# Hash attention and a gated feed-forward on one core: a hash ahead of scores, a norm's products on another engine, turns and hashes at other steps

## The chip, the core and the metric

The kernel runs on one core of a Trainium2 chip. The core has a matrix engine (PE; its weight loads are listed apart as PEld), a vector engine (DVE), a scalar engine (ACT), GpSimd (POOL) and a sync engine (SP), which here only issues DMAs. Each works through its own list of instructions in the order of the program; semaphores hold an instruction until what it needs is there. The metric is the device time of one execution in microseconds.

## What is computed

Two parts follow each other. The first is attention with a mask from hashing: each query and each key of 64 numbers is projected on 6 directions, the 6 signs make a bucket, and a query sees only the keys of its own bucket. The second is a feed-forward with a norm ahead of it, a gate and a value.

```python
q_bits = (einsum('bhsd,dk->bhsk', q, proj) > 0)      # q, k, v: 4 x 8 x 768 x 64
k_bits = (einsum('bhsd,dk->bhsk', k, proj) > 0)      # proj: 64 x 6
mask = q_bucket[:, :, :, None] == k_bucket[:, :, None, :]
scores = where(mask, q @ k.T / sqrt(64), -1e9)
x = softmax(scores) @ v                              # to 3072 x 512
xn = x / sqrt(mean(x * x) + 1e-6) * rms_g
out = (silu(xn @ w_gate) * (xn @ w_val)) @ w_out     # 512 -> 1536 -> 512
```

## The kernel before, in words

**Units and steps.** The 3072 tokens are eight units `u` of 384 (`HALF`), two for each batch `b`. A unit has 8 heads, in four pairs `hp`. One step is a third of a head's scores for one unit: two matmuls into a bank pair (`scores`, L321) and one exponential on ACT (`probs`, L333). There are 24 steps to a unit (`NS`), 192 in all. In step `t` the program issues the scores of step `t + 1`, the exponential of step `t`, and then whatever the table `plan[t]` holds, in the order in which it was put there with `at(w, s, f, ...)`. So the order on every engine is written out by hand: `plan` decides, and each engine follows its own share of it. Scores have two buffers, so those of step `t + 1` wait for the exponential of step `t - 1`. The first ten heads in `order` are two of u = 0, two of u = 1, then the other six of u = 0; the rest follow unit by unit.

**Keys and queries.** A pair's q and k come in naturally and are turned, either by PE (`turn_pe`, L150, copied out of its bank by DVE or ACT, L152) for batch 0 and the pairs (1,0) and (1,1), or by DVE block transposes (`turn_dve`, L176 and L183) for the rest. POOL casts them to 16 bits (L166, L196). The hash projects the turned tensors on PE (`d_ps`; L229 in `hash_pairs`, L204 in `hash_half`), DVE takes the signs (`bits`, L212), and they are put below q and k as further rows of the 16-bit operand `QK`, so that one matmul gives score and mask at once. They get there by DVE copies (`move`, L251) or by DMAs from SP (`send`, L258 and L261; `hash_one`, L219 and L280). The dictionary `spots` lists, for each pair that DVE turns, the step of its load, the steps of the turns of k and q (each a part), and the step of its hash.

**Attention and norm.** `av` (L346) multiplies the probabilities with v into `o_ps`, which has one buffer per pair of heads. `attn_out` adds a correction and copies out (DVE, `otmp`, L360), takes the reciprocal (L365), scales (POOL, `x`, L367) and squares (POOL, `sq`, L372). `sumsq` sums the squares (DVE, L376). `norm` adds up the four pairs (`ss`, L386), takes the power -1/2 on POOL (`rstd`, L390) and scales into 16 bits on DVE (`xn`, three instructions, L393). `turn_x` transposes on PE (`x_ps`, L400) and multiplies by the norm's weights on DVE (`xnT`, L406).

**Feed-forward.** `gate` and `value` (`feed`, L417) go through 12 tiles of 128 columns; ACT takes a tanh (L425), DVE two products (`a` and `ht`, L434 and L435). `project` (L446) sums into `y_ps`, `store` copies it out on ACT (L458) and issues the DMA (L459). `spread` distributes these pieces and the hashes that are due over a unit's 24 steps by fixed costs. The banks of `t_ps`, `d_ps`, `x_ps`, `g_ps`, `v_ps` and `y_ps` are three in all, of one tag.

**Zeros.** `idle` (L517) multiplies zeros: matmuls whose result nobody reads. There are eight ahead of the first work, three ahead of the first hash, two ahead of the first scores, two ahead of the second head's hash, and four in steps 37 and 38.

**DMA order.** SP takes its DMAs in the program's order, loads, sends and stores alike. Loaded tiles share a ring of eight buffers, so a load can wait for the last reader of an older tile.

Of the kernel before, what the change touches and what calls it, by code (L numbers as in the profile page):

```python
# [15 lines left out]
H = 8  # L16
# [15 lines left out]
def kernel(  # L32
# [12 lines left out]
    nc = tc.nc  # L45
# [114 lines left out]
    def turned(b, hp, which):  # L160
        return (qT if which == "q" else kT)[b, hp].rearrange("p (h c) -> p h c", h=2)
# [48 lines left out]
    def signs(bt, ps, c0, n):  # L210

        nc.vector.tensor_scalar(  # L212
            out=bt[0:n, 1, c0 : c0 + HALF], in0=ps[0:n], scalar1=0.0, scalar2=0.5,
            op0=ALU.is_gt, op1=ALU.subtract,
        )
# [21 lines left out]
    def hash_direct(b, hp, heads):  # L237


        where = [(which, hh) for which in "kq" for hh in heads]  # L240
        pss = hash_pairs([turned(b, hp, which)[:, hh, :] for which, hh in where])
        bt = spool.tile([128, 2, S], FP16, name="bits")

        def sign(e):
            signs(bt[:, :, e * HALF :], pss[e], 0, 32 * len(where))

        def move(e, kinds="kq", n=1, only=heads):
            for t, (which, hh) in enumerate(where):
                if which in kinds and hh in only:
                    o = (0 if which == "q" else S) + e * HALF  # L250
                    nc.vector.tensor_scalar_mul(  # L251
                        QK[b, 2 * hp + hh, "h"][64:KROWS0, o : o + n * HALF],
                        bt[32 * t : 32 * t + 6, 1, e * HALF : (e + n) * HALF],
                        4.0 * BIT * BIT if which == "k" else 1.0,
                    )

        def send():
            nc.vector.tensor_scalar_mul(bt[:, 0, :], bt[:, 1, :], own)  # L258
            for t, (which, hh) in enumerate(where):
                o = 0 if which == "q" else S  # L260
                nc.sync.dma_start(  # L261
                    out=QK[b, 2 * hp + hh, "h"][64:KROWS0, o : o + S],
                    in_=bt[32 * t : 32 * t + 6, 0, :],
                )

        return sign, move, send
# [47 lines left out]
    def scores(u, i):  # L314
        b, half = divmod(u, 2)
        h, ch = divmod(i, 3)
        rows = KROWS0 if (b, h // 2) in ONPE else KROWS
        ps = scps.tile([128, 2, 512], FP32, name="s_ps")
        for j in range(2):
            jt = 2 * ch + j  # L320
            nc.tensor.matmul(  # L321
                ps[:, j, 0:HALF],
                QK[b, h, "h"][0:rows, S + jt * 128 : S + (jt + 1) * 128],
                QK[b, h, "h"][0:rows, half * HALF : (half + 1) * HALF],
                start=True, stop=True,
            )
        sps[u, i] = ps
# [23 lines left out]
                skip_group_check=True,  # L351
            )

    def attn_out(u, hp):
        b = u // 2
        if hp == 0:
            x[u] = xpool.tile([128, 3, DMODEL], FP32, name="x")
        o = ot.pop((u, hp))
        tmp = spool.tile([128, 3, 2, 66], FP32, name="otmp")
        nc.vector.tensor_add(  # L360
            tmp[:, :, :, 0:65], o[:, :, :, 0:65],
            cvb[b % 2][:, 2 * hp : 2 * hp + 2, 0:65].unsqueeze(1).to_broadcast([128, 3, 2, 65]),
        )
        r = spool.tile([128, 3, 2, 1], FP32, name="rcp")
        nc.vector.reciprocal(r, tmp[:, :, :, 64:65])  # L365
        xd = x[u][:, :, 128 * hp : 128 * hp + 128]
        nc.gpsimd.tensor_mul(  # L367
            xd.rearrange("p c (h d) -> p c h d", h=2), tmp[:, :, :, 0:64],
            r.to_broadcast([128, 3, 2, 64]),
        )  # L370
        sq = spool.tile([128, 3, 128], FP32, name="sq")
        nc.gpsimd.tensor_mul(sq, xd, xd)  # L372
        return sq

    def sumsq(u, hp, sq):
# [4 lines left out]

    ht, gts = {}, {}

    def norm(u):

        ss = spool.tile([128, 3], FP32, name="ss")
        nc.vector.tensor_reduce(  # L386
            out=ss, in_=ssp[u % 2].rearrange("p h c -> p c h"), op=ALU.add, axis=AX.X
        )
        rstd = spool.tile([128, 3], FP32, name="rstd")
        nc.gpsimd.tensor_tensor(out=rstd, in0=ss, in1=mhalf, op=ALU.pow)  # L390
        xn[u] = npool.tile([128, 3, DMODEL], FP16, name="xn")
        for c in range(3):
            nc.vector.tensor_scalar_mul(xn[u][:, c, :], x[u][:, c, :], rstd[:, c : c + 1])  # L393
# [119 lines left out]
    def idle(n, new=None):  # L513

        ps = new("z_ps") if new else wz
        for _ in range(n):
            nc.tensor.matmul(ps, zeros16[:, 0:128], zeros16, start=True, stop=True)  # L517
# [17 lines left out]
    def at(w, s, f, *a):  # L535
        plan[NS * w + s].append(lambda: f(*a))
# [3 lines left out]
    turn_pe(0, 0, 0, "q", act=(0,))  # L540
    cast_part(0, 0, "k", 1, 0, 1)
    turn_pe(0, 0, 1, "k")
    idle(3)
    sign, move, _ = hash_direct(0, 0, (0,))
    turn_pe(0, 0, 1, "q", nc.scalar.copy)
    idle(2)
# [4 lines left out]
    sign(1)  # L551
    move(1, "k")
    scores(0, 0)


    def second_head():
        idle(2)
        sign1, move1, _ = hash_direct(0, 0, (1,))
        sign1(0)
        move1(0)  # L560
        sign1(1)
        move1(1, "k")
        move(1, "q")
        move1(1, "q")

    moves = {}

    def hash_pair(b, hp):
        sign, *moves[b, hp] = hash_direct(b, hp, (0, 1))
        sign(0)  # L570
        sign(1)

    def move_pair(b, hp, hh):
        moves[b, hp][0](0, n=2, only=(hh,))
# [1 line left out]
    def send_pair(b, hp):  # L576
        moves[b, hp][1]()

    at(0, 0, second_head)
    at(0, 1, v_prep, 0, 0)  # L580
    at(0, 1, cast_part, 0, 0, "q", 1)
# [26 lines left out]
    for hp, ts in ((0, (8, 22, 23, 24, 25, 24, 26, 26, 28, 42)), (1, (12, 27, 28, 29, 30, 29, 41, 32, 33, 43))):  # L608
        tl, ts = ts[0], ts[1:]
        for w in "kq":  # L610
            at(0, tl, load_natural, nc.sync, 1, hp, w)
        at(0, tl, load_v, nc.sync, 1, hp)
        at(0, ts[0], new_pair, 1, hp)
        for t, hh, w in zip(ts[0:4], (0, 1, 0, 1), "kkqq"):
            at(0, t, turn_pe, 1, hp, hh, w)
        at(0, ts[4], cast_pool, 1, hp, "k")
        at(0, ts[5], cast_pool, 1, hp, "q")
        at(0, ts[6], hash_pair, 1, hp)
        at(0, ts[7], send_pair, 1, hp)
        at(0, ts[8], v_prep, 1, hp)  # L620
        at(2, 3 + 6 * hp, v_mean, 1, hp, 2, range(6))

    spots = {
# [10 lines left out]
    }  # L634
    sqs = {}

    def o_step(u, hp):
        sqs[u, hp] = attn_out(u, hp)

    def s_step(u, hp):  # L640
        sumsq(u, hp, sqs.pop((u, hp)))

    at(0, 24, nc.gpsimd.tensor_scalar_mul, gcol, gcol, float(DMODEL) ** 0.5)
    at(0, 36, norm, 0)
    at(0, 37, idle, 2, bank)
    at(0, 38, idle, 2, bank)
    for c in range(3):
        at(0, 38, turn_x, 0, c)
    for n, (u, h) in enumerate(order):
        for part in range(2):  # L650
            at(0, 3 * n + 4 + part, av, u, h, part)
        if h % 2:
            at(0, 3 * n + 5, o_step, u, h // 2)
            at(0, 3 * n + (10 if h < 7 else 8 if u == 0 else 7), s_step, u, h // 2)

# [30 lines left out]
    for u in range(7):  # L686
        gates = [
            (FEED, f is gate and part == 0, [(0, f, u, ft, part)])
            for ft in range(NF) for f in (gate, value) for part in range(2)
        ]  # L690
        if u == 0:
            t0 = 40
            spread(t0, 2 * NS - t0, gates)
            continue
        t0 = NS * (u + 1)
        at(0, t0 + 4, norm, u)
        pieces = []
        for i in range(9):
            c, n = divmod(i, 3)
            steps = [(0, project, u - 1, c, 4 * n, 4 * n + 4)]  # L700
            if n == 2:
                steps.append((1, store, u - 1, c))
            pieces.append((4 * PROJ, True, steps))
            if i in (6, 7):
                pieces += [
                    (TURN, False, [(0, turn_x, u, c)]) for c in ((0,), (1, 2))[i - 6]
                ]
        spread(t0, NS, pieces + gates)
# [86 lines left out]
```

## Time and profile before

| What | Value |
|---|---|
| Time, median of 3 runs | 346.39 us (346.1 to 346.78) |
| The profiled execution | 346.98 us, span of its instructions 345.2 us |
| PE busy | 331.2 us, 96% of the span |
| DVE, ACT, POOL busy | 249.8, 225.7, 147.8 us |
| Chain that ended last | PE 80%, DVE 9%, POOL 4%, issue 4%, ACT 2% |
| Exponential, 128x768 (L333) | 192 times, 899 ns each |
| Scores matmul (L321) | 384 times, 326 ns each |
| Scale on POOL (L367) / square on POOL (L372) | 32 times each, 829 / 826 ns |
| Sum of squares on DVE (L376) | 32 times, 528 ns |

A row of the timeline has the start in the span, the length, the engine, the line, the operation, the tiles written and read, and how many alike follow each other; in square brackets stands how long the engine was idle before it and who ended that. The lengths of matmuls overlap, since they are pipelined: what one costs is the distance between starts. A row of the waits has the total, the number and the longest. "Issue" is time for which the profile shows no wait.

### The profile page before, as it was taken

Reading aid. Unit: us, or ns where it says so; the run is one execution under the profiler, and the core shown is the slowest. Engines: PE = TensorE matmul, PEld = TensorE weight load, DVE = VectorE, ACT = ScalarE, POOL = GpSimd, SP = SyncE. Lnnn points to the kernel's source line nnn. Section 1 sums busy time; section 2 is a strip of 40 time slices with the busy share of each in tenths; the row PEclk is TensorE's granted clock in tenths of the full one; section 3 lists DMA queues with packets and bytes.
Section 4 is the critical chain, followed back from the end, with each engine's and each line's share of the span. In section 5 each row is a group of like instructions: output and inputs, shape, how many; then the busy total and the mean of one; then the engine's idle time right before and its main releaser. Section 6 shows DMA issues by size and latency. Waiting matters only on the chain.

```text
span 345.2 us, 7819 instructions
## 1 busy us (share of the span) xinstructions
PE 331.2 (96%) x3035; PEld 198.6 (58%) x3035; DVE 249.8 (72%) x521; ACT 225.7 (65%) x327; POOL 147.8 (43%) x210
## 2 busy tenths in 40 slices
PE   8798978998999999999899999999999999999996
PEld 4455745654656556565556556565556656664554
DVE  2669967777798857987798757988796546674870
ACT  2689984666566667776577767776667767863322
POOL 4389966306354443637453623646460121112000
PEclk9999999999999999999999999999999999999999
DMA  7899955910276925270827016200200010001002
GB/s 248 279 201 293 202 113 75 211 41 30 34 179 98 186 69 104 73 140 10 162 82 133 9 65 116 59 7 9 93 6 4 3 61 32 2 0 63 31 0 93
DMA packets 79029, 31.21 MB, mean 90 GB/s; under 512 B 64928, under 2 KB 75024, under 8 KB 78992
## 3 DMA queue, kind: packets, MB, share of 16 engines
q1 hardware_dynamic: 75888, 25.73, 30.9%
q0 software_dynamic: 2656, 4.72, 7.8%
q8 instruction: 24, 0.39, 0.5%
q10 hardware_dynamic: 448, 0.27, 0.2%
q14 instruction: 13, 0.11, 0.1%
HBM read 28.32 MB, written 6.29 MB: 100 GB/s over the span
## 4 chain that ended last, share of the span: by engine, by line
PE 80%; DVE 9%; POOL 4%; issue 4%; ACT 2%; DVEq 0%; POOLq 0%
PE v_ps L417 17%; PE g_ps L417 17%; PE s_ps L321 15%; PE y_ps L446 13%; PE o_ps L346 9%; PE t_ps L150 2%; PE d_ps L204 2%; PE d_ps L229 2%; PE x_ps L400 2%; DVE xn L393 2%; PE z_ps L517 1%; ACT psb L333 1%; DVE bits L212 1%; POOL rstd L390 1%; POOL x L367 1%
## 5 line engine op out<-in xcount | busy, mean ns | idle before, releaser
L333 ACT ACTIVATE psb<-s_ps,ebias 128x768 f16<-128x768 f32 x192 | 168.1, 899 | 29.8 <-PE s_ps L321 28.5
L321 PE MATMUL s_ps<-QK 76*128 76x384 f16 (+1 forms) x384 | 93.6, 326 | 3.6 <-ACT psb L333 1.2
L425 ACT ACTIVATE t<-g_ps 128x384 f32<-128x384 f32 x96 | 47.1, 490 | 57.7 <-PE g_ps L417 56.9
L417 PE MATMUL g_ps<-xnT,wg 128*128 128x384 f16 x384 | 82.1, 325 | 0.1
L417 PE MATMUL v_ps<-xnT,wv 128*128 128x384 f16 x384 | 80.9, 325 | 0.2 <-DVE a L434 0.2
L367 POOL TENSOR_TENSOR x<-otmp,rcp 128x384 f32<-128x384 f32 x32 | 26.5, 829 | 113.1 <-DVE rcp L365 112.6
L434 DVE SCALAR_TENSOR_TENSOR a<-t,g_ps 128x384 f32<-128x384 f32 x96 | 52.6, 548 | 25.3 <-ACT t L425 23.4
L446 PE MATMUL y_ps<-wo,ht 128*128 128x512 f16 x276 | 68.0, 378 | 0.0
L346 PEld LDWEIGHTS <-psb 128*128 128x128 f16 x1152 | 51.8, 97 | 20.8 <-issue 5.0
L435 DVE SCALAR_TENSOR_TENSOR ht<-a,v_ps 128x384 f16<-128x384 f32 x96 | 53.2, 554 | 11.0 <-PE v_ps L417 1.9
L346 PE MATMUL o_ps<-vl,psb 128*128 128x65 f16 x1152 | 56.3, 193 | 2.6 <-DVE otmp L360 2.5
L321 PEld LDWEIGHTS <-QK 76*128 76x128 f16 (+1 forms) x384 | 34.3, 98 | 34.9 <-issue 9.3
L417 PEld LDWEIGHTS <-wv 128*128 128x128 f16 x384 | 35.2, 97 | 22.4 <-issue 1.6
L417 PEld LDWEIGHTS <-wg 128*128 128x128 f16 x384 | 34.7, 97 | 21.1 <-DVE xnT L406 0.6
L446 PEld LDWEIGHTS <-ht 128*128 128x128 f16 x276 | 24.7, 97 | 22.5
L372 POOL TENSOR_TENSOR sq<-x 128x384 f32<-128x384 f32 x32 | 26.4, 826 | 2.5
L458 ACT COPY ysb<-y_ps 128x512 f32<-128x512 f32 x23 | 13.5, 585 | 18.5 <-PE y_ps L446 18.4
L376 DVE TENSOR_REDUCE ssp<-sq 128x3 f32<-128x384 f32 x32 | 16.9, 528 | 10.6 <-POOL sq L372 10.4
L360 DVE TENSOR_TENSOR otmp<-o_ps,cvb 128x390 f32<-128x390 f32 x32 | 17.9, 558 | 8.3 <-PE o_ps L346 8.1
L196 POOL CAST QK<-qT 64x768 f16<-64x768 f32 x20 | 16.6, 832 | 16.7 <-DVE qT L183 15.3
L196 POOL CAST QK<-kT 64x768 f16<-64x768 f32 x20 | 16.7, 833 | 13.9 <-DVE kT L183 9.2
L393 DVE TENSOR_SCALAR xn<-x,rstd 128x512 f16<-128x512 f32 x24 | 14.1, 643 | 7.8 <-POOL rstd L390 7.8
(74 smaller groups left out, 279.5 us busy)
## 6 DMA issues: line engine op xcount, KB each, us to landing
vn<-in_v_dram SPq DMA_DIRECT2D x16, 384.0 KB
out_dram<-ysb SPq DMA_DIRECT2D x23, 256.0 KB
qL<-in_q_dram SPq DMA_DIRECT2D x40, 96.0 KB
kL<-in_k_dram SPq DMA_DIRECT2D x40, 96.0 KB
kn<-in_k_dram SPq DMA_DIRECT2D x5, 384.0 KB
qn<-in_q_dram SPq DMA_DIRECT2D x5, 384.0 KB
wg<-in_moe_w_gate_dram POOLq DMA_DIRECT2D x2, 768.0 KB, 9.7
wv<-in_moe_w_val_dram POOLq DMA_DIRECT2D x2, 768.0 KB, 9.6
```

Source lines behind the costliest of these rows:

```text
L196: nc.gpsimd.tensor_copy(QK[b, 2 * hp + hh, "h"][0:64, o : o + S], src[64 * hh : 64 * hh + 64, :])
L321: nc.tensor.matmul(ps[:, j, 0:HALF], QK[b, h, "h"][0:rows, S + jt * 128 : S + (jt + 1) * 128], QK[b, h, "h"][0:rows, half * HALF : (half + ...
L333: nc.scalar.activation(psb[u, h][:, 2 * ch : 2 * ch + 2, :], sps.pop((u, i))[:, :, 0:HALF], AF.Exp, bias=ebias, scale=ESCALE,)
L346: nc.tensor.matmul(o[:, c, hh, 0:65], psb[u, h][:, jt, c * 128 : (c + 1) * 128], vls[b % 2][:, h, 2 * (jt % 3) + jt // 3 if b in PARITY el ...
L367: nc.gpsimd.tensor_mul(xd.rearrange("p c (h d) -> p c h d", h=2), tmp[:, :, :, 0:64], r.to_broadcast([128, 3, 2, 64]),)
L372: nc.gpsimd.tensor_mul(sq, xd, xd)
L393: nc.vector.tensor_scalar_mul(xn[u][:, c, :], x[u][:, c, :], rstd[:, c : c + 1])
L417: nc.tensor.matmul(ps, w[:, kt, fs], xnT[u][:, kt, :], start=(kt == 0), stop=(kt == 3))
L425: nc.scalar.activation(t, fbank[u, ft, "g_ps"], AF.Tanh, scale=0.5)
L434: nc.vector.scalar_tensor_tensor(out=a, in0=t, scalar=1.0, in1=g, op0=ALU.add, op1=ALU.mult)
L435: nc.vector.scalar_tensor_tensor(out=ht[u][:, ft, :], in0=a, scalar=0.5, in1=vv, op0=ALU.mult, op1=ALU.mult)
L446: nc.tensor.matmul(y, ht[u][:, ft, c * 128 : (c + 1) * 128], wo[:, ft, :], start=(ft == 0), stop=(ft == NF - 1),)
```

## The change

1. *The start.* One zero instead of three ahead of the first hash. The second head's hash matmuls are issued straight behind the first scores; the two zeros ahead of it are gone.
2. *The first norm.* For the last pair of u = 0, `attn_out` scales and squares on DVE; the sum of squares, the total and the power follow at once, in step 32, behind the attention matmuls. The hash of pair (1,1) moves behind them, from step 32 to 33, its signs after the total, its send from 33 to 34. `xn` is formed in step 33's list, the transposes stand in step 37 instead of 38, with three zeros instead of four, and the gates of u = 0 begin in step 38 instead of 40.
3. *Turns and hashes.* (1,2): turns in steps 48 and 49 instead of 48 to 51, hash at 50 instead of 52. (2,0) and (2,1) are loaded two steps earlier. (2,3): turns from 96, 96, 97, 97, 99, 99, 105, 105 to 96, 97, 99, 105, 105, 106, 106, 107, hash from 106 to 108. (3,3) likewise 48 steps later. (3,0): turns up to two steps later, hash at 118 instead of 117.

```diff
-    def attn_out(u, hp):
+    def attn_out(u, hp, eng=nc.gpsimd):
...
-        nc.gpsimd.tensor_mul(
+        eng.tensor_mul(
             xd.rearrange("p c (h d) -> p c h d", h=2), tmp[:, :, :, 0:64],
             r.to_broadcast([128, 3, 2, 64]),
         )
         sq = spool.tile([128, 3, 128], FP32, name="sq")
-        nc.gpsimd.tensor_mul(sq, xd, xd)
+        eng.tensor_mul(sq, xd, xd)
...
-    def norm(u):
+    rstds = {}
+
+    def norm_scale(u):
...
         nc.gpsimd.tensor_tensor(out=rstd, in0=ss, in1=mhalf, op=ALU.pow)
+        rstds[u] = rstd
+
+    def norm(u):
+        if u not in rstds:
+            norm_scale(u)
+        rstd = rstds.pop(u)
...
-    idle(3)
+    idle(1)
     sign, move, _ = hash_direct(0, 0, (0,))
...
     scores(0, 0)
+    sign1, move1, _ = hash_direct(0, 0, (1,))
     def second_head():
-        idle(2)
-        sign1, move1, _ = hash_direct(0, 0, (1,))
         sign1(0)
...
-        at(0, ts[6], hash_pair, 1, hp)
-        at(0, ts[7], send_pair, 1, hp)
+        if hp == 0:
+            at(0, ts[6], hash_pair, 1, hp)
+            at(0, ts[7], send_pair, 1, hp)
...
-        (1, 2): (20, (48, 49), (50, 51), 52),
+        (1, 2): (20, (48, 48), (49, 49), 50),
         (1, 3): (45, (57, 58), (59, 60), 61),
-        (2, 0): (52, (63, 64, 65, 66), (67, 69, 70, 71), 73),
-        (2, 1): (61, (72, 73, 75, 81), (82, 83, 84, 85), 86),
+        (2, 0): (50, (63, 64, 65, 66), (67, 69, 70, 71), 73),
+        (2, 1): (59, (72, 73, 75, 81), (82, 83, 84, 85), 86),
         (2, 2): (70, (87, 88, 89, 90), (91, 93, 94, 95), 97),
-        (2, 3): (84, (96, 96, 97, 97), (99, 99, 105, 105), 106),
-        (3, 0): (93, (107, 108, 109, 111), (112, 113, 114, 115), 117),
+        (2, 3): (84, (96, 97, 99, 105), (105, 106, 106, 107), 108),
+        (3, 0): (93, (108, 109, 111, 112), (113, 114, 115, 117), 118),
...
-        (3, 3): (132, (144, 144, 145, 145), (147, 147, 153, 153), 154),
+        (3, 3): (132, (144, 145, 147, 153), (153, 154, 154, 155), 156),
     }
+    TX = 37
...
-    at(0, 36, norm, 0)
-    at(0, 37, idle, 2, bank)
-    at(0, 38, idle, 2, bank)
-    for c in range(3):
-        at(0, 38, turn_x, 0, c)
...
+            if (u, h) == (0, H - 1):
+
+                at(0, 3 * n + 5, o_step, u, h // 2, nc.vector)
+                at(0, 3 * n + 5, s_step, u, h // 2)
+                at(0, 3 * n + 5, norm_scale, u)
+                at(0, 3 * n + 6, hash_only, 1, 1)
+                at(0, 3 * n + 6, hash_signs, 1, 1)
+                at(0, 3 * n + 6, norm, u)
+                at(0, 3 * n + 7, send_pair, 1, 1)
+                at(0, TX - 1, idle, 2, bank)
+                at(0, TX, idle, 1, bank)
+                for c in range(3):
+                    at(0, TX, turn_x, u, c)
+                continue
...
-            t0 = 40
+            t0 = TX + 1
             spread(t0, 2 * NS - t0, gates)
```

`hash_only` issues the hash matmuls of a pair, `hash_signs` its two sign instructions; together they are the old `hash_pair`.

More of the change, by code (lines that the diff above doesn't have):

```diff
@@ L566, with hash_only, hash_signs @@
     moves = {}
+    pair_signs = {}
+    def hash_only(b, hp):
+        pair_signs[b, hp], *moves[b, hp] = hash_direct(b, hp, (0, 1))
+    def hash_signs(b, hp):
+        for e in range(2):
+            pair_signs[b, hp](e)
     def hash_pair(b, hp):
-        sign, *moves[b, hp] = hash_direct(b, hp, (0, 1))
-        sign(0)
-        sign(1)
+        hash_only(b, hp)
+        hash_signs(b, hp)
     def move_pair(b, hp, hh):
@@ L623, with o_step @@
     spots = {
[1 row of a table removed]
[1 row of a table added]
         (1, 3): (45, (57, 58), (59, 60), 61),
[2 rows of a table removed]
[2 rows of a table added]
         (2, 2): (70, (87, 88, 89, 90), (91, 93, 94, 95), 97),
[2 rows of a table removed]
[2 rows of a table added]
         (3, 1): (102, (120, 121, 123, 129), (130, 131, 132, 133), 134),
         (3, 2): (114, (135, 136, 137, 139), (140, 141, 142, 143), 145),
[1 row of a table removed]
[1 row of a table added]
     }
+    TX = 37
     sqs = {}
-    def o_step(u, hp):
-        sqs[u, hp] = attn_out(u, hp)
+    def o_step(u, hp, *eng):
+        sqs[u, hp] = attn_out(u, hp, *eng)
     def s_step(u, hp):
@@ L652 @@
         if h % 2:
+            if (u, h) == (0, H - 1):
[11 more added lines that the diff above has]
+                continue
             at(0, 3 * n + 5, o_step, u, h // 2)
-            at(0, 3 * n + (10 if h < 7 else 8 if u == 0 else 7), s_step, u, h // 2)
+            at(0, 3 * n + (10 if h < 7 else 7), s_step, u, h // 2)
     SCORES, AV, PROJ, FEED, TURN, HASH = 330, 290, 216, 324, 220, 1000
```

## The prediction

> **What bounds the kernel now.** I read the page's busy shares first, then the waits of the matmul engine, then the timeline where those waits lie. First the busy shares of the page, then who PE waited for (in us: total, times, longest).
>
> ```profile
> PE 331.2 (96%) x3035; PEld 198.6 (58%) x3035; DVE 249.8 (72%) x521; ACT 225.7 (65%) x327; POOL 147.8 (43%) x210
> ```
>
> ```profile
> PE o_ps L346 <- DVE otmp L360: 2.5, 3, 0.9
> PE x_ps L400 <- DVE xn L393: 1.6, 3, 0.9
> PE x_ps L400 <- DVE bits L212: 1.4, 1, 1.4
> PE s_ps L321 <- ACT psb L333: 1.2, 3, 0.8
> PE s_ps L321 <- issue: 1.2, 2, 0.8
> ...
> PE s_ps L321 <- DVE QK L251: 1.0, 2, 0.7
> ```
>
> PE is the bound: idle 14.0 of 345.2 us. What it waits for is few and short, so a change can gain only at the places where these waits lie, plus the zero matmuls, which are busy but not work. By PE's timeline they are: 0.31, 0.72 and 0.84 us before 14 us; 0.63, 0.77, 0.33 and 0.94 around the first norm (47 to 55); 1.36, 0.87 and 0.41 at the transposes of the norms of u = 1, 3 and 5 (86.4, 166.0, 243.8). Between 55 and 310 us there are besides these only two of 0.2, so PE time won early should be kept to the end. The change goes to exactly these places.
>
> **The start.** Timeline rows (start, length, engine, line, what; in brackets the idle time before and what ended it):
>
> ```profile
> 7.58 0.51 PE L229 MATMUL d_ps<-kT,pj 64*32 64x384 f32 x2
> 11.02 0.32 PE L321 MATMUL s_ps<-QK 70*128 70x384 f16 x1 [0.72 <-DVE QK L251]
> 11.19 0.59 PE L517 MATMUL z_ps<-zeros 128*128 128x512 f16 x2
> 11.71 0.51 PE L229 MATMUL d_ps<-kT,pj 64*32 64x384 f32 x2
> 13.83 0.48 PE L321 MATMUL s_ps<-QK 70*128 70x384 f16 x2 [0.84 <-issue]
> 14.35 1.69 ACT L333 ACTIVATE psb<-s_ps,ebias 128x768 f16<-128x768 f32 x2 [0.42 <-PE s_ps L321]
> ```
>
> The second head's hash stands behind the second scores, which wait for a DVE copy until 11.02, and behind two zeros. It ends at 12.6, then come its signs (0.55) and two moves (0.53) on DVE, and only then the fourth scores at 13.83. In the new order it follows the first scores at once. By hand with these rows:
> - Two of three zeros before the first hash go. It then waits for the copy of kT (6.73 + 0.56 = 7.29) and starts at about 7.35 instead of 7.58: 0.23 earlier, as are the first scores (9.66 to 9.43).
> - Second hash at 9.43 + 0.32 + 0.09 (the drain seen from zeros to hash) = 9.84 instead of 11.71. Its banks are free: the first signs end near 8.8, the copy of qT near 9.2.
> - Second scores 10.62 and 10.79; exponentials at 11.15, then 0.80 apart (the spacing of ACT's back-to-back pairs): 11.95.
> - Signs at 10.74, moves to 11.86. The fourth scores now wait for the bank of the second (exponential ends 12.05) instead: 12.1. The fourth exponential is at 12.75, ACT's own pace, instead of 14.35.
>
> Gain 1.6. What is late next is ACT, so no more than this can come. Everything behind shifts alike, as the loads that it needs were early: by the queue's bytes, k of pair (0,1) has landed before 7 and is used at 14. Bounds: 0.4 (the two zeros of 0.216 alone) to 1.8 (DVE's and PE's own shift, were ACT not there).
>
> [...] Three transposes take 0.85 us at 4.56 and 0.49 at 14.15; the zeros come 0.43 apart until 6.9 and 0.216 from 8.75, so the rate rises near 7.0, within the zeros that go. In the new kernel PE is busy from 1.18 to 6.9 without a hole, and then idle 0.44. I take the rise as unmoved.
>
> [...]
>
> **The first norm.**
>
> ```profile
> 47.17 0.19 DVE L365 RECIPROCAL rcp<-otmp 128x6 f32<-128x6 f32 x1
> ...
> 47.51 0.84 POOL L367 TENSOR_TENSOR x<-otmp,rcp 128x384 f32<-128x384 f32 x1 [1.54 <-DVE rcp L365]
> 48.43 0.82 POOL L372 TENSOR_TENSOR sq<-x 128x384 f32<-128x384 f32 x1
> 49.28 0.55 DVE L376 TENSOR_REDUCE ssp<-sq 128x3 f32<-128x384 f32 x1 [1.62 <-POOL sq L372]
> ...
> 50.13 0.89 POOL L390 TENSOR_TENSOR rstd<-ss,mhalf 128x3 f32<-128x3 f32 x1 [0.88 <-DVE ss L386]
> ...
> 51.05 1.28 DVE L393 TENSOR_SCALAR xn<-x,rstd 128x512 f16<-128x512 f32 x3 [1.00 <-POOL rstd L390]
> ```
>
> The chain is serial, and PE has too little else to do: that is the 2.7 us of holes and the four zeros. Two multiplications move from POOL (0.84, 0.82) to DVE. No row shows an f32 product of two SBUF tensors there; the nearest are the reduction over the same 384 elements (0.53) and otmp (0.56 for 390). I take 0.55; bounds 0.53 and 0.84. [...]
>
> Also the pair's attention matmuls come before the hash of pair (1,1) instead of behind it, and that hash's signs go behind the sum of squares, into the time of the power. In the clock of before: last attention matmuls 44.56 to 45.0 (were 45.46 to 45.9), otmp 45.05, rcp 45.64, x 45.87, sq 46.45, reduction 47.03, ss 47.6, power 47.86 to 48.73; signs (1.02 for both) 47.8 to 48.8 beside it; xn 48.85 to 50.13 instead of 51.05 to 52.33. PE meanwhile does five scores (0.33 each), the hash, two half heads (0.27 each) and three zeros, held twice by ACT, and is at its transposes at 49.25; they start 0.54 after xn, at 49.4. It is free at 51.27 and waits for xnT: xn ends 50.13, the multiplication of the hash for the send comes first (0.38 by its row at 47.28), then 1.88 as before: 52.4. First gate at 52.45 instead of 54.91. By then PE has done two scores and one half head less (0.93), and the hash is now inside. **Gain** 54.91 - 52.45 - 0.93 = 1.5. Bounds: 0.4 (multiplications at POOL's price, send at 0.9), 2.3 (no wait for xnT).
>
> The gates start two steps earlier, 48 pieces over ten steps instead of eight: the same PE work. The eight sends queue on SP some 3 us later, and behind them the loads of (1,3), needed near 90 us and issued from 54: covered.
>
> **Norms of u = 1, 3, 5.**
>
> ```profile
> 86.36 0.38 PE L400 MATMUL x_ps<-ident,xn 128*128 128x128 f16 x4 [1.36 <-DVE bits L212]
> ```
>
> ```profile
> 164.96 2.38 DVE L393 TENSOR_SCALAR xn<-x,rstd 128x512 f16<-128x512 f32 x3 [0.97 <-POOL rstd L390]
> ```
>
> ```profile
> 164.88 1.78 POOL L196 CAST QK<-kT 64x768 f16<-64x768 f32 x2
> ```
>
> u = 1: the transposes wait for a bank that the hash of (1,2) holds until its signs, which stand behind all three xn. The hash moves two steps ahead of the norm, so that wait (1.36) goes. New: the four turns stand closer, and by their spacing the last ends at 78.9, while PE reaches the hash at 78.5. I take 0.45 for that; net 0.9, bounds 0.3 and 1.36. The xn stay slow, as POOL still casts beside them.
>
> u = 3 and 5: xn takes 1.04 beside POOL's casts and 0.43 without (norm of u = 0). Three turns leave the stretch ahead of the norm, one of them (0.35) ahead of otmp, and the casts of k that ran beside xn now come behind a turn of step 105. First xn then ends near 165.1, and PE is free at 165.17: the 0.87 goes, likewise the 0.41. Bounds 0.6 to 1.28 together.
>
> What they pay: in steps 105 to 107 and 153 to 155 five turns (0.43 each) stand where two stood. DVE's rows there have idle stretches of 0.1 to 0.4; I take 0.2 in all, up to 1.0. The hash of (2,3) moves from step 106 to 108, scores at 113: PE's rows leave some 7 us from hash to scores; pair (1,3) needed 5.9 (98.39 to 104.27) with no wait. On SP the load of v of (3,1) now waits for a turn of step 107; behind it are one store, whose three buffers last until 199, and the sends of that hash, which are later anyway.
>
> **Sum.** 1.6 + 1.5 + 0.9 + 1.28 - 0.2 = 5.1 us. The profiled execution took 346.98 (span 345.2 and 1.8 around it), so 341.9; the median of the runs shown, 346.39, is 0.6 below it: 341.3. Holes refill in part, so I say 341.5.
>
> **Rivals.**
> - [...] Chance 0.10.
> - *New waits.* DVE is late after the crowded turns, the sends of (2,3) and (3,3) land after their scores; each late us is a us of PE. Slack about 1 us; with 1 to 1.5 lost at each place and at step 50: 343.5 to 345. Chance 0.10.
> - *Slower: the rate stays low.* Without the four zeros at the start PE is busy, by the times above, about 60% in 7 to 17 us; if that no longer lifts the rate, each us of PE work costs two. The gain of 5.1 is lost when some 5 us of work is done at half rate, that is when the rise comes later than about 17.5; at 20, 347.5. Against: around the first norm PE has 2.7 us of holes in 8 and the rate holds (matmuls of 512 columns stay 0.216 apart). Chance 0.07.
>
> The forecast, 340.2 to 342.8, has 0.70; the last 0.03 are gains given back exactly. The range reaches into the new waits: 340.2 to 344.4. About 0.2% (0.7 us) is what a measurement of this kernel can tell from no change. Faster 0.90, same 0.03, slower 0.07.
>
> **What would show it.** Start: second hash near 9.8, the fourth exponential near 12.75, zeros at 0.216 from 8.5 on. First norm: x and sq at 0.55 on DVE, first gate 4 us earlier than 54.91. Norms: no wait over 0.2 at the x_ps of u = 1, 3, 5; a wait of up to 0.45 at the hash of step 50; xn at 0.43 for u = 3 and 5. Wrong if transposes at 8 us take 0.85 for three, or if PE has waits for QK or g_ps near 175 and 255.

## The result and the profile after

| | Before | Changed |
|---|---|---|
| Median of the timed runs (four each) | 346.41 us (346.10 to 346.78) | 344.56 us (344.26 to 344.89) |
| Profiled execution (span) | 346.98 us (345.2) | 344.45 us (342.6) |

The ratio is 0.9946, with an interval of 0.9929 to 0.9964: the change makes the kernel 1.85 us faster. The direction was right, the size was not: 5 us had been forecast, and the time lies 0.2 us above the top of the range.

In the changed kernel the lines from L393 on have moved by 8: `xn` is L401, the transposes L408, `xnT` L414, gate and value L425, the zeros L525. First the busy shares of its page, then who PE waited for (total, times, longest, in us).

```profile
PE 329.6 (96%) x3030; PEld 197.7 (58%) x3030; DVE 249.2 (73%) x523; ACT 225.6 (66%) x327; POOL 146.3 (43%) x208
```

```profile
PE s_ps L321 <- DVE QK L251: 1.9, 2, 1.7
PE s_ps L321 <- DMA QK<-bits: 1.2, 1, 1.2
...
PE g_ps L425 <- DVE xnT L414: 0.8, 1, 0.8
PE v_ps L425 <- DVE a L442: 0.8, 2, 0.6
...
PE x_ps L408 <- DVE xn L401: 0.3, 1, 0.3
```

The old waits at `x_ps` (1.6 and 1.4) and two of three at `o_ps` are gone or short. In their place stand three that the forecast did not have: 1.7 for a copy on DVE at the start (0.7 before), 1.2 for a DMA that brings hash rows, 0.8 for `a`, a product of the gates.

The start of each exponential, before and after, tells where these lie. There are 192 in each trace, one per step, so the difference of the n-th is the gain won by then. This is worked out from the starts in the two timelines; a minus is earlier.

| Up to step | Difference (us) | What lies since the line above |
|---|---|---|
| 3 | -1.49 | the start |
| 33 | -1.46 | nothing |
| 48 | -3.11 | the first norm: 1.65 won |
| 60 | -4.20 | the norm of u = 1: 1.09 won (first 0.45 lost, then 1.54 won) |
| 66 | -2.90 | first scores of pair (1,3): 1.30 lost |
| 99 | -2.89 | nothing |
| 105 | -3.54 | the norm of u = 3: 0.65 won |
| 114 | -2.64 | the steps behind it: 0.90 lost |
| 123 | -2.28 | 0.36 lost |
| 159 | -2.69 | the norm of u = 5: 0.42 won |
| 189 | -2.64 | nothing |

**The start.** The timeline of the changed kernel, PE's rows and then DVE's (start, length, engine, line, what; in brackets the idle time before).

```profile
9.08 0.51 PE L229 MATMUL d_ps<-kT,pj 64*32 64x384 f32 x2
9.10 0.51 PE L229 MATMUL d_ps<-qT,pj 64*32 64x384 f32 x2
...
9.87 0.82 PE L321 MATMUL s_ps<-QK 70*128 70x384 f16 x4
12.34 0.48 PE L321 MATMUL s_ps<-QK 70*128 70x384 f16 x2 [1.65 <-DVE QK L251]
```

```profile
9.98 0.55 DVE L212 TENSOR_SCALAR bits<-d_ps 64x384 f16<-64x384 f32 x1 [0.50 <-PE d_ps L229]
10.57 1.67 DVE L251 TENSOR_SCALAR QK<-bits 6x384 f16<-6x384 f16 x2
12.27 0.55 DVE L212 TENSOR_SCALAR bits<-d_ps 64x384 f16<-64x384 f32 x1
```

The hash starts at 9.08, even earlier than forecast (9.84). But the two moves of its signs take 1.67 us together, where the forecast had 0.53. Beside them on POOL:

```profile
10.41 0.82 POOL L289 CAST vl<-vn 128x768 f16<-128x768 f32 x1 [1.39 <-DMA vn<-in_v_dram]
11.30 0.83 POOL L166 CAST QK<-qT 64x768 f16<-64x768 f32 x1
```

By the trace's single ends, the casts end at 11.24 and 12.13 and the moves at 11.35 and 12.24: each move ends 0.11 us behind the cast that ran beside it. The fourth exponential is at 12.86 (12.75 was forecast), but held by DVE and not by ACT, so that the two times agree by chance.

**The first norm.** DVE's rows of the changed kernel, then PE's first gate.

```profile
44.16 0.19 DVE L365 RECIPROCAL rcp<-otmp 128x6 f32<-128x6 f32 x1
44.39 0.56 DVE L367 TENSOR_TENSOR x<-otmp,rcp 128x384 f32<-128x384 f32 x1
44.98 0.56 DVE L372 TENSOR_TENSOR sq<-x 128x384 f32<-128x384 f32 x1
...
47.41 1.28 DVE L401 TENSOR_SCALAR xn<-x,rstd 128x512 f16<-128x512 f32 x3
48.60 0.42 DVE L258 TENSOR_SCALAR bits<-bits,own 128x768 f16<-128x768 f16 x1
48.93 1.88 DVE L414 TENSOR_TENSOR xnT<-x_ps,gcol 128x512 f16<-128x512 f16 x3
```

```profile
50.87 0.65 PE L425 MATMUL g_ps<-xnT,wg 128*128 128x384 f16 x3 [0.85 <-DVE xnT L414]
```

The products take 0.56 each (0.55 was taken). The first gate was forecast for 52.45 in the clock of before; less the 1.5 won at the start, that is 50.95, and it starts at 50.87.

**Norms of u = 1, 3, 5.** At u = 1 no wait is left. The hash of step 50 shows no idle time either, but its last matmuls wait for the last turn of q: from its first matmul to the next scores pass 1.22 us (75.27 to 76.49) instead of 0.78. At u = 3 `xn` is as short as hoped, and the transposes still wait a little:

```profile
161.98 1.28 DVE L401 TENSOR_SCALAR xn<-x,rstd 128x512 f16<-128x512 f32 x3 [0.97 <-POOL rstd L392]
```

```profile
162.53 0.40 PE L408 MATMUL x_ps<-ident,xn 128*128 128x128 f16 x4 [0.33 <-DVE xn L401]
...
178.58 0.81 PE L425 MATMUL v_ps<-xnT,wv 128*128 128x384 f16 x4 [0.63 <-DVE a L442]
```

The second row is the price: DVE has turns, the signs and products of the hash that moved to step 108, a sum and `otmp` in a row from 174.54 to 178.01, and is late with `a`. A second wait for `a` follows further on:

```profile
189.59 0.23 PE L305 MATMUL m_ps<-vsum,ones 128*128 128x130 f16 x1 [0.20 <-DVE a L442]
```

Counted as distances between starts, PE loses 0.83 and 0.36 at these two places against before, nearly all of the 0.90 and 0.36 of the table.

**The wait for the DMA.** The sends of the hash rows of pair (1,3) in SP's queue, before and after (an "x4" row spans four issues; the last row before and the first row after are single issues out of four):

```profile
94.91 2.99 SPq L117 DMA_DIRECT2D kL<-in_k_dram  x4
97.94 0.64 SPq L103 DMA_DIRECT2D vn<-in_v_dram  x1
98.69 0.87 SPq L459 DMA_DIRECT2D out_dram<-ysb  x2
101.14 3.41 SPq L280 DMA_DIRECT2D QK<-bits  x4
104.60 0.64 SPq L117 DMA_DIRECT2D qL<-in_q_dram  x1
```

```profile
91.77 2.57 SPq L117 DMA_DIRECT2D qL<-in_q_dram  x1
94.45 2.66 SPq L117 DMA_DIRECT2D kL<-in_k_dram  x4
97.20 0.58 SPq L103 DMA_DIRECT2D vn<-in_v_dram  x1
97.89 3.40 SPq L280 DMA_DIRECT2D QK<-bits  x4
```

Before, SP was free when the signs came (101.08), and the load of pair (2,1) was issued behind the sends, from 104.60. After, that load is due two steps earlier, ahead of the sends, and SP is still issuing it when the signs are ready at 96.89: the first send goes out a full microsecond late. It took a slow issue as well: the 2.57 us of the first row stand where the other parts of that load take 0.6 to 1.0. With 0.65 there, SP would have been free near 95.9, ahead of the signs. e3 and e4, which keep the load at 59, have such an issue of 2.0 and 2.3 us at the same place; what held it, no run here shows. The first send's packets also begin later, 2.06 us behind the issue instead of 1.52. The second send, on which the first scores hang, lands at 100.81, and PE:

```profile
101.37 0.48 PE L321 MATMUL s_ps<-QK 76*128 76x384 f16 x2 [1.19 <-DMA QK<-bits]
```

Before there was no wait, but no slack either: signs at 101.08, data of the second send landed at 103.83, its last semaphore update at 104.14, scores at 104.27. Those 0.13 us from the last update to the scores are the same in the changed kernel (101.24 and 101.37), where PE does wait.

### The profile page after: what moved, and what is told of

Same layout as the page of the kernel before. It is cut to its first block, busy times and chain, and to the rows that moved or that the text cites. A ratio compares the mean times of both kernels' runs of the same rounds, so it can differ in the third digit from the quotient of the medians.

```text
span 342.6 us, 7811 instructions
## 1 busy us (share of the span) xinstructions
PE 329.6 (96%) x3030; PEld 197.7 (58%) x3030; DVE 249.2 (73%) x523; ACT 225.6 (66%) x327; POOL 146.3 (43%) x208
## 4 chain that ended last, share of the span: by engine, by line
PE 84%; DVE 10%; ACT 2%; issue 2%; POOL 1%; DMA 1%; DVEq 0%; SPq 0%; POOLq 0%
PE v_ps L425 17%; PE g_ps L425 17%; PE s_ps L321 16%; PE y_ps L454 16%; PE o_ps L346 9%; PE d_ps L204 2%; PE t_ps L150 2%; PE d_ps L229 2%; PE x_ps L408 1%; ACT psb L333 1%; DVE xnT L414 1%; PE m_ps L305 1%; DVE a L442 1%; PE z_ps L525 1%; DVE QK L251 1%
## 5 line engine op out<-in xcount | busy, mean ns | idle before, releaser
L425 PE MATMUL g_ps<-xnT,wg 128*128 128x384 f16 x384 | 82.5, 325 | 1.0 <-DVE xnT L414 0.8
L425 PE MATMUL v_ps<-xnT,wv 128*128 128x384 f16 x384 | 81.6, 325 | 0.9 <-DVE a L442 0.8
L367 POOL TENSOR_TENSOR x<-otmp,rcp 128x384 f32<-128x384 f32 x31 | 25.7, 830 | 98.8 <-DVE rcp L365 98.3
L425 PEld LDWEIGHTS <-wv 128*128 128x128 f16 x384 | 35.2, 97 | 23.3 <-issue 2.5
L425 PEld LDWEIGHTS <-wg 128*128 128x128 f16 x384 | 34.7, 97 | 21.9 <-issue 0.9
L372 POOL TENSOR_TENSOR sq<-x 128x384 f32<-128x384 f32 x31 | 25.7, 828 | 2.4
L414 DVE TENSOR_TENSOR xnT<-x_ps,gcol 128x512 f16<-128x512 f16 x23 | 15.1, 686 | 5.9 <-PE x_ps L408 5.9
```

Source lines behind the costliest of these rows:

```text
L367: eng.tensor_mul(xd.rearrange("p c (h d) -> p c h d", h=2), tmp[:, :, :, 0:64], r.to_broadcast([128, 3, 2, 64]),)
L372: eng.tensor_mul(sq, xd, xd)
L414: nc.vector.tensor_mul(dst, ps, gcol.unsqueeze(2).to_broadcast([128, 4, 128]))
L425: nc.tensor.matmul(ps, w[:, kt, fs], xnT[u][:, kt, :], start=(kt == 0), stop=(kt == 3))
```

## The experiments

"Ratio" is against the kernel before, beside which each was run. All build on the changed kernel, but for two that build on the one before.

### The loads ahead of the sends

**e1_load61**: the load of (2,1) goes back.

```diff
-        (2, 1): (59, (72, 73, 75, 81), (82, 83, 84, 85), 86),
+        (2, 1): (61, (72, 73, 75, 81), (82, 83, 84, 85), 86),
```

> The changed kernel with one number back: the loads of pair (2,1) issued in step 61 again, behind the sends of the hash of (1,3), instead of in step 59, ahead of them. Theory (SP's order): in the changed kernel SP issued the first send at 97.89, 1.0 us after its data were ready, as it was still at the loads, its packets took 2.1 us instead of 1.5, and the scores stood still for 1.19 us. Then that wait goes and the time falls by 1.2 us, to about 343.3. Rival (DVE late: the signs themselves come too late for the scores, whatever SP does): the wait stays, no change.

342.66 us (six runs), ratio 0.9899 (0.9874 to 0.9923). The DMA is gone from PE's waits, and between steps 60 and 66 nothing is lost any more (-4.30 and -4.32). The place of one load, two steps earlier, costs the change 1.3 us by the trace, 1.6 by the ratios and 1.9 by the medians.

**e2_only_load59**: the kernel before, with that load at 59 as its only change (the same line, 61 to 59).

> The kernel before with one edit only: the loads of (2,1) issued in step 59 instead of 61. Theory (SP's order): the sends of (1,3) landed 0.44 us ahead of their scores there, so about 1 us of delay shows nearly whole: slower by 0.7 to 1.3 us. Rival (DVE): no change. A third answer, no change with the sends late, would mean that the wait of the changed kernel comes from scores that arrive earlier.

354.79 us, ratio 1.024 (1.0222 to 1.0258), far more than expected. PE's waits, and the trace cut into stretches (length; busy time and instructions of each engine; granted clock, DMA share, GB/s):

```profile
PE s_ps L321 <- DMA QK<-bits: 6.5, 1, 6.5
```

```profile
101.00:108.27 7.27, 2.58 (x27) 1.42 (x24) 3.04 (x7) 2.30 (x4) 2.43 (x3) 1.00 0.90 172
108.27:115.10 6.83, 4.99 (x24) 2.65 (x25) 1.54 (x3) 1.28 (x2) 0.00 (x0) 0.50 0.53 103
115.10:122.00 6.90, 6.89 (x69) 4.49 (x68) 5.72 (x14) 4.97 (x8) 3.30 (x4) 1.00 0.53 110
```

The mechanism holds; the wait is 6.5 us here and 1.2 in the changed kernel, and more stands in the queue: the load of (2,0) is still at 52, two steps later than in the changed kernel, so that both loads stand ahead of the sends, from 90.28 to 106.36. The loss is 6.5 us of waiting, and behind it 6.83 us at half the clock, which cost another 2.5 (from step 59 to 75 the difference grows by 9.0).

### The turns

**e3_old_turns** and **f1_load61_old_turns**: the changed kernel, and e1, with the old spots of (2,3), (3,0) and (3,3).

```diff
-        (2, 3): (84, (96, 97, 99, 105), (105, 106, 106, 107), 108),
-        (3, 0): (93, (108, 109, 111, 112), (113, 114, 115, 117), 118),
+        (2, 3): (84, (96, 96, 97, 97), (99, 99, 105, 105), 106),
+        (3, 0): (93, (107, 108, 109, 111), (112, 113, 114, 115), 117),
...
-        (3, 3): (132, (144, 145, 147, 153), (153, 154, 154, 155), 156),
+        (3, 3): (132, (144, 144, 145, 145), (147, 147, 153, 153), 154),
```

> The changed kernel with the turns and hashes of (2,3), (3,0) and (3,3) at their old steps; the rest stays. The forecast (turns ahead of the norms cost 1.28 us of waiting, crowding them later costs 0.2): slower by 1.1 us. Theory from the two traces (what the norms of u = 3 and 5 gain, 0.9 us, is lost again behind them in steps 105 to 125, where products of DVE come late to PE): same, or faster by up to 0.3 us.

> The kernel e1_load61 with the turns and hashes of (2,3), (3,0), (3,3) at their old steps, so that no wait for the sends of (1,3) blurs the answer. Forecast: slower than e1_load61 (342.7) by 1.1 us. Theory (0.96 us of waits at the norms of u = 3 and 5 is gained, 0.8 to 1.0 us is lost where the crowded turns make DVE late): between 0 and 0.4 us slower, 342.7 to 343.1; the wait at the transposes of u = 3 is 0.9 us again and the wait of v_ps for DVE near 178 us is gone.

e3: 344.50 us (twelve runs), ratio 0.997 (0.9941 to 0.9998); f1: 342.83 (seven), ratio 0.9918 (0.9888 to 0.9947). That is 0.06 below the changed kernel and 0.17 above e1: the moved turns, worth 1.1 us in the forecast, are worth nothing that can be told. In f1 the wait at `x_ps` for `xn` is back, and the one at `v_ps` for `a` is down from 0.8 to 0.2: the one was bought with the other.

```profile
PE x_ps L408 <- DVE xn L401: 1.3, 2, 0.9
...
PE v_ps L425 <- DVE a L442: 0.2, 1, 0.2
```

Both kernels scatter. The profiled execution of f1 was one of its three longest (345.5 us), and shows why. Its stretches, and PE's rows:

```profile
5.00:12.00 7.00, 5.19 (x36) 2.30 (x35) 4.82 (x11) 3.44 (x6) 3.66 (x6) 1.00 1.01 327
12.00:19.00 7.00, 6.71 (x40) 4.97 (x40) 2.52 (x7) 4.55 (x7) 2.88 (x4) 0.51 0.69 219
19.00:26.00 7.00, 6.61 (x96) 4.17 (x96) 4.98 (x12) 5.82 (x9) 4.58 (x7) 1.00 1.04 210
```

```profile
12.29 0.80 PE L321 MATMUL s_ps<-QK 70*128 70x384 f16 x2 [1.13 <-DVE QK L251]
12.88 0.85 PE L150 MATMUL t_ps<-ident,kn 128*128 128x128 f32 x3
...
20.23 0.49 PE L150 MATMUL t_ps<-ident,kn 128*128 128x128 f32 x3
```

From 12.2 to 19.0 the clock is at half, the same three transposes taking 0.85 instead of 0.49, and 2.4 us are lost from step 3 to step 33. This comes close to the slower rival of the prediction, in single executions: that had the rate stay low, here it rose and fell back.

**f4_old_turns_late_casts**: f1, with the casts on POOL that fall into a unit's first steps put behind the norm by one step more.

```diff
-        return t - t % NS + 7 if 2 <= t % NS < 7 else t
+        return t - t % NS + 8 if 2 <= t % NS < 8 else t
```

> The kernel f1_load61_old_turns with one further edit: casts and preparations that fall into the steps behind a norm move to step 8 of their unit instead of 7, in POOL's order behind the next scale and square, which wait for attention. Theory (the 1.04 us of each xn instead of 0.43 at u = 3 and 5 comes from POOL's casts beside it): the waits at the transposes of u = 3 and 5 fall from 0.9 and 0.4 us to 0.4 and 0, without crowded turns; faster than f1 by 0.6 to 1.0 us. Rival (the turns ahead of the norm are what makes it late): xn at 0.43 but the waits stay, no change.

341.71 us, ratio 0.9877 (0.9849 to 0.9905), 1.1 below f1. `xn` at u = 3 takes 1.28 for three (2.39 in f1), the wait at `x_ps` is 0.3, and nothing is given back: -4.28 at step 99, -4.84 at 105 and still at 114, -5.40 at 159. So `xn` was slow for the casts alone. To move them was enough, and the turns had not to be touched.

**g4_hash12_at_51**: e1, with the hash of (1,2) one step later, out of the way of its last turn.

```diff
-        (1, 2): (20, (48, 48), (49, 49), 50),
+        (1, 2): (20, (48, 48), (49, 49), 51),
```

> The kernel e1_load61 with the hash of (1,2) in step 51 instead of 50. In the changed kernel PE is held about 0.45 us at that hash, since the last turn ends at 75.67 and PE is there at 75.3. Theory: that goes, faster by 0.2 to 0.45 us. Rival (the signs then stand closer to the norm's sum, and the transposes of u = 1 wait instead): no change or slower, with a wait of x_ps near 82 us.

342.83 us, ratio 0.99 (0.9884 to 0.9916): no change from e1. PE's row at the norm of u = 1 says why: the 0.45 at the hash has become

```profile
83.91 0.38 PE L408 MATMUL x_ps<-ident,xn 128*128 128x128 f16 x4 [0.44 <-DVE xnT L414]
```

### The first norm

**g3_products_on_pool**: e1, with the scale and the square back on POOL, and the new order kept.

```diff
-                at(0, 3 * n + 5, o_step, u, h // 2, nc.vector)
+                at(0, 3 * n + 5, o_step, u, h // 2)
```

> The kernel e1_load61 with the last pair of u = 0 scaled and squared on POOL again; its order and steps stay new. By the rows of the changed kernel DVE takes 0.56 for each and POOL 0.83. Theory (the chain from that pair to the first gate binds PE): slower by 0.5 to 0.8 us, 343.2 to 343.4, and the wait of g_ps for xnT grows from 0.85 to about 1.4 us. Rival (the order is what gained 1.6 us there, the engine nothing): no change.

343.42 us, ratio 0.9917 (0.9904 to 0.9931): 0.76 above e1 by the medians. From step 33 to 48 it wins 0.94 where the changed kernel wins 1.65. The engine is worth about 0.7, the rest of the change there (the order of hash and attention, and one zero less) the other 0.9.

### The start

**e4_old_start** and **f2_load61_old_start**: the changed kernel, and e1, with the old start.

```diff
-    idle(1)
+    idle(3)
...
-    sign1, move1, _ = hash_direct(0, 0, (1,))
     def second_head():
+        idle(2)
+        sign1, move1, _ = hash_direct(0, 0, (1,))
```

> The changed kernel with the old start: three zeros ahead of the first hash, the second head's hash behind the second scores and two zeros. Forecast: slower by 1.6 us. Theory (the profiled executions differ in when PE's rate rises, near 7.0 us before and near 4.2 us after, and in the new order two moves on DVE take 0.8 us instead of 0.3 beside POOL's casts): slower by 0.5 to 1.0 us only, and the part of 1.49 us beyond that was the earlier rise.

> The kernel e1_load61 with the old start. Forecast: slower by 1.6 us, 344.3. Theory (the executions profiled so far differ by up to 1.2 us in the old start alone, by when PE's rate rises; with that averaged the new order is worth 0.7 to 1.1 us): 343.4 to 343.8.

e4: 345.21 us (twelve runs), ratio 0.9965 (0.9948 to 0.9982); f2: 343.30, ratio 0.9909 (0.9894 to 0.9924). Both lose 0.65 to their pair by the medians (0.66 and 0.35 by the ratios, whose intervals overlap), not 1.5. The traces tell why. The clock rose at different times in the profiled executions, between 4.3 and 7.2 us in those named here, by the distances of transposes and zeros, and the profiled execution of before is the one at 7.2. With the old start the fourth exponential came at 14.35 there, but at 13.19 in e4 (rise at 4.8) and 13.04 in f2 (4.5). With the new start it is at 12.86 in the changed kernel (4.3), 12.80 in e1 (5.9), 12.35 in e3 (4.5) and 13.13 in f1 (5.3). So most of the 1.49 was that one execution's late rise.

**f3_load61_v_first**: e1, with the first load of v ahead of the second one of q, so that POOL casts v earlier.

```diff
-    load_natural(nc.sync, 0, 1, "q")
     load_v(nc.sync, 0, 0)
+    load_natural(nc.sync, 0, 1, "q")
```

> The kernel e1_load61 with the load of v of pair (0,0) issued one place earlier, ahead of the load of q of pair (0,1). Theory (POOL casts that v when it lands, and two moves of 6 rows on DVE beside it take 0.8 us each instead of 0.25; so the fourth scores wait for DVE up to 1.65 us): the cast runs ahead of the moves, the fourth scores come 0.4 to 0.8 us earlier, and the time falls by as much. Rival (ACT's pace of 0.80 us binds there, as the forecast had it): no change. If q of (0,1) lands late, PE waits at its transposes near 14 us and it is slower.

342.34 us, ratio 0.9883 (0.9866 to 0.99), 0.32 below e1. DVE's rows of f3:

```profile
9.32 0.68 DVE L251 TENSOR_SCALAR QK<-bits 6x384 f16<-6x384 f16 x1
10.07 0.55 DVE L212 TENSOR_SCALAR bits<-d_ps 64x384 f16<-64x384 f32 x1
10.66 0.53 DVE L251 TENSOR_SCALAR QK<-bits 6x384 f16<-6x384 f16 x2
```

The same two moves take 0.53, no longer held up by two casts (POOL's now run from 9.06 and 9.95). Instead the move ahead of them, which stands beside the first of these casts, takes 0.68 (0.25 in the changed kernel, with POOL idle) and ends 0.11 us behind it. PE's fourth scores now wait for ACT (0.76), as the prediction had it, and the fourth exponential is at 12.08. That the two moves were long for the casts beside them is settled (1.67 us with them, 0.53 without); its worth is a third to half a microsecond, since other waits take part of the 0.7.

**g1_late_casts_v_first** joins f3's edit to f4; **g2_zeros_in_holes** adds zeros to g1 where PE waits at the start.

> The two gains together: old turns, (2,1) loaded in step 61, casts in step 8 behind a norm, and v of (0,0) loaded ahead of q of (0,1). Theory (they lie at different places and add): 341.7 - 0.3 to 0.5 = 341.2 to 341.4, fourth exponential near 12.1 us. Rival (an earlier start meets a later wait, at the sends of a hash for instance): 341.7. Some executions should again show a granted clock of 0.99 and be 2 to 3 us longer, as 9 of 39 with the new start so far.

> The kernel g1_late_casts_v_first with zeros where PE waits anyway: three instead of one ahead of the first hash, and four in step 1, ahead of the fourth scores. Theory (the missing zeros leave PE too idle between 5 and 12 us in some executions, and its rate then falls back to half for 6.8 us): no execution below 0.998 of the clock; median within 0.3 us of g1, as the zeros stand in holes. Rival (the fall-back is chance and has nothing to do with the zeros): the same share, about one in four, at 0.99. If the four zeros stand in the way of the fourth scores, 0.2 to 0.5 us slower.

```diff
-    idle(1)
+    idle(3)
...
+    at(0, 1, idle, 4)
```

g1: 341.45 us, ratio 0.986 (0.9843 to 0.9876). g2: 341.36, ratio 0.9856 (0.9838 to 0.9874). Both beat both kernels, by some 4.7 and 3.1 us; between them no difference can be told.

### Zeros and the clock

**h1_old_order_fewer_zeros** is the kernel before without the four zeros that the change drops at the start; **h2_load61_zeros_in_holes** is e1 with g2's zeros; **h3_load61_no_zeros** is e1 without the zero ahead of the first hash and the two ahead of the first scores.

```diff
-    idle(3)
+    idle(1)
...
-        idle(2)
```

```diff
-    idle(1)
...
-    idle(2)
```

> The kernel before with the four zeros of the start taken out and nothing else: the second head's hash stays behind the second scores. Forecast (by its bounds): faster by at least 0.4 us, the two zeros on the chain. Theory (PE waits for DVE at the first hash anyway, so only the two zeros ahead of the second hash count, and PE is emptier): faster by 0.3 to 0.6 us in most executions; and if the missing zeros are what lets the rate fall back, some executions at a clock of 0.99 that the kernel before does not have (its lowest is 0.995).

> The kernel e1_load61 with three zeros ahead of the first hash and four in step 1, in the hole ahead of the fourth scores. Theory (zeros keep the rate up): no execution below 0.998, median 342.4 to 342.8. Rival (fall-backs have another cause): executions at 0.99 to 0.995 as before, one in five.

> The kernel e1_load61 without any zeros between the first eight and step 36: also the one ahead of the first hash and the two ahead of the first scores go. Theory (zeros keep the rate up): far more than one execution in five at 0.99 or lower, median 343.5 to 345.5 with a wide spread. Rival (chance): the same share as e1_load61, median 342.4 to 342.9, as these zeros stand in holes.

h1: 346.14 us (twelve runs), ratio 0.9992 (0.9971 to 1.0013): over all executions no difference. But in its seven executions with a mean granted clock of 0.998 or more the median is 345.81, and 346.47 in the eleven such of the kernel before: 0.66 less, as much as the whole start in e4. In h1's trace the clock rose at 4.3, as in that of the changed kernel, and the fourth exponential is at 12.54, 0.32 earlier than with the new order. So the zeros left out can account for what the start gains at full clock; that the new order adds to it, while its moves run into the casts, is not shown. In f3, where they do not, the fourth exponential is at 12.08 with a rise at 4.5, so there the order seems to gain.

h2: 342.88, ratio 0.9884 (0.9862 to 0.9906), with six runs within 0.16 us. h3: 343.80, ratio 0.9914 (0.9882 to 0.9946): three runs of six at 342.7 to 342.8 with the full clock, three at 344.8 to 345.4 with a mean granted clock of 0.99. Such executions, at 0.995 or below, were 9 of 54 in the kernels with the new start and its zeros, 0 of 10 with zeros in the holes (g2, h2), 0 of 18 with the old start on the new kernel (e4, f2), 5 of 12 in h1, and 15 of 63 in the kernel before (6 of the 17 beside h1), there never below 0.995. That fewer zeros make the fall likelier fits h3. h1 does not show it, but for one execution at 0.99. And the kernel before has all its zeros and loses clock in one execution of four, so the zeros of the start are not the whole story; no trace here shows where it does. These counts are too small to give a rate.

## Why the prediction came out 3 us low

| Step of the prediction | Forecast | Trace of after | By undoing it on the chip |
|---|---|---|---|
| The start, zeros and order together | 1.6 | 1.49 | 0.65 (e4, f2) |
| The first norm | 1.5 | 1.65 | 0.76 for the engine alone (g3) |
| The norm of u = 1 | 0.9 | 1.09 | not undone |
| Turns: won at u = 3 and 5 | 1.28 | 1.07 | nothing in sum (e3, f1) |
| Turns: price | -0.2 | -1.26 | |
| Load ahead of the sends of (1,3) | nothing | -1.30 | -1.3 to -1.9 (e1) |

With the start at 0.65 the trace's column sums to 1.9; measured were 1.85, which is closer than the terms are known. The steps that failed, the largest first:

- **"The sends ... and behind them the loads ... : covered."** This looked at loads behind sends, and never at sends behind loads. Of (2,0) and (2,1), "loaded two steps earlier", the working priced nothing. It took pair (1,3)'s 5.9 us from hash to scores "with no wait" as a measure of slack, when the last of these was a send that landed 0.44 us before the scores started, and whose last semaphore update came 0.13 us before. The new-waits rival had the kind of loss right ("land after their scores") and gave 343.5 to 345; it looked for it at (2,3) and (3,3), and had 0.10.
- **The turns' price, "0.2 in all, up to 1.0".** It is 1.26, and eats the gain. The idle stretches of 0.1 to 0.4 on DVE were counted as room, but `a` and `ht` come there in a chain with ACT and PE, and turns and signs in front of them make PE's next `v_ps` wait. What the step wanted, an `xn` free of POOL's casts, came as forecast (0.48 instead of 1.04), and f4 gets it without the price.
- **The start, "Gain 1.6".** Two errors, that all but cancel in the one trace. The moves were costed at 0.53 from a row with an idle POOL, and run into casts: 1.67, so that DVE and not "ACT's own pace" holds the fourth scores. And the rows were those of an execution whose clock rose late (7.2 us); the sum put "the rise as unmoved" and took the whole distance as gain. Against the medians the start is worth 0.65, and h1 has as much from the zeros alone, for which the prediction had 0.4 as its lower bound. The sum then took off 0.6 more, the distance of that execution from the median; if the late rise made that distance, it was counted twice.

The rows of the moves agree with each other: a move that began beside a running cast ended 0.11 us behind it, once in the trace of before (10.88 behind 10.76), twice in the changed kernel (11.35 and 12.24 behind 11.24 and 12.13) and once in f3. These four took 0.66 to 0.86 us; with POOL idle a move took 0.25. What ties a move's end to the cast's, no run here shows.

What was right: the first norm (1.5 against 1.65, its first gate to 0.1 us), the products' 0.55, the norm of u = 1 with its 0.45 at the hash, and that PE time won early is kept: between the places of the table the difference stands still for up to 30 steps.

Of the other rivals, the slower one's half rate exists (f1, from 12.2 to 19.0 us). The executions at a mean granted clock of 0.995 or below, 9 of the 54 with the new start and its zeros, lie 1.2 to 3.5 us above their kernel's median, and did not move the median of the changed one. A late rise of the clock is what before's own profile already had, with 7.2 us. What stays open is how the start's 0.65 divides between zeros, order and chance: single pairs of executions give from -0.1 to 0.8 at the fourth exponential.

## What to carry to other kernels

Where an engine issues loads and small urgent sends in one queue, an earlier load is a later send (here by 1.0 us, with 1.2 us of waiting on PE): for every DMA that moves, list what now stands behind it and how long before its use that landed, from the landing and not from the distance between instructions. Leave room for slow issues: the one here took 2.57 us, where the median of the 80 load parts in the same trace is 0.64. Cost a small DVE copy from a row that has the same neighbour on POOL (here 0.66 to 0.86 us beside a cast, 0.25 with POOL idle). And before a gap at the start is counted as gain, look at what the clock did in that one execution (here it rose at 7.2 us before and at 4.3 after).

## What the runs showed of the hardware

- The clock rose at 7.2 us in the profiled execution of before, and at 4.8 and 4.5 us in those of e4 and f2, which have the same start; with the new start at 4.3 us (the changed kernel), 5.9 (e1), 4.5 (e3) and 5.3 (f1). What sets the time, no run here shows.
- The clock fell to half for 6.83 us in e2 (0.50 from 108.27 to 115.10) and for some 6.8 us in f1 (0.51 from 12 to 19). In e2 a wait of 6.5 us stood ahead; in f1 PE had been busy for 5.19 of 7.0 us, with no hole over 1.2 us just ahead, while a hole of 1.65 us at the same place left the changed kernel's clock at full. What makes it fall, no run here shows.
- A send of a few rows took 2.7 to 2.9 us from its group's first issue to the landing of the second (101.14 to 103.83 before, 97.89 to 100.81 after), with 0.78 to 0.89 us for each issue on SP.
